# A fused attention and SoLU kernel: the first two tiles' h spread over rounds 10 to 14, one product moved, two g_ln products on VectorE, w_out copies later

## Chip, core and metric

The kernel runs on one core of a Trainium2 chip. The metric is device microseconds of one execution, lower is better. Engines are named as in the profile: PE is TensorE (PEld its weight loads), DVE VectorE, ACT ScalarE, POOL GpSimd, SP SyncE, which here issues nearly every DMA.

## What is computed

```python
# attention, per batch (8) and head (8), seq 576, head_dim 64
scores = q @ k.T / 8
scores = where(scores >= max(scores) - tau, scores, -1e9)
attn   = exp(scores - max(scores)); attn /= sum(attn) + 1e-9
x      = (attn @ v), heads side by side          # 4608 tokens x 512
# feed forward, per token
h    = x @ w_in                                   # 512 -> 1024
solu = h * exp(h - max(h)) / (sum(...) + 1e-9)
ln   = (solu - mean) / sqrt(var + 1e-6) * g_ln
out  = ln @ w_out                                 # 1024 -> 512
```

w_in and w_out arrive as 64-bit floats, and the kernel makes 32-bit floats of them with integer operations on the engines.

## The kernel before, in words

Attention is cut into 144 slots, 18 for each batch: two heads by 128 query rows each, and two slots at a batch's end for the 64 rows that are left over. A Python loop runs over rounds (line 855): round r issues the scores of slot r and the later steps of earlier slots, so the order of the instructions on every engine is the order in which the loop calls them. Each engine works its own list from front to back and waits on semaphores where data comes from another.

A slot goes through these steps. `scores(r)` (line 411): PE makes two 128 by 576 tiles in PSUM (`s0`, `s1`), ahead of them, where due, the turns of the next batch's q and k by matmuls with an identity (line 379). `maxes(r)` (line 455): DVE finds row minima of the negated scores. `ramp` (line 470) and `exps` (line 479): ACT, two of each. `keeps` (lines 388, 390): copies of turned q and k from PSUM. In round r+1: `normalise(r)` on POOL (lines 486 to 491), `blocks(r)` on DVE (line 501, 32x32 transposes), and after every second slot three DMAs (lines 510, 512) that carry T into wT. Three or four rounds after its second slot, the product with v (`attend_steps`, line 542) runs on PE for both slots of a unit, and ACT copies it to `xh` (line 572). `pv_due` holds the round from which each product is due, in order; slots 8 and 9 are due in round 12.

When the four units of 256 tokens of a batch and kind are done, two tiles of 128 tokens are ready for the feed-forward. Before the change, `ff_h` makes h in two halves, one per round: half 0 writes with `part` 0, then a memset on POOL (`fence`, line 110) waits for the last four matmuls of that half, and the first matmul of half 1 waits for that memset, since the rows change banks there. Half 0 of the first tile, (0, 0, 0), comes in round 11 and half 1 in round 12; the second, (0, 0, 1), has rounds 13 and 14. h takes one of two PSUM pairs (`p0`, `p1`), which the products with v and the output use too, and holds it until `ff_mul`. After h: `ff_max` (DVE, line 620), `ff_exp` (ACT, 629), `ff_mul` (DVE, 635), `ff_sum` (POOL, 640), `ff_stats` (DVE 650, then small POOL operations 654 to 661 whose last result is nb), `ff_norm` (ACT, 671, writes V), `ff_norm2` (DVE, 676), `ff_swap` (four DMAs, 687), `ff_turn` (DVE, 697, writes uT), `ff_o` (PE, 710, in two halves), `ff_store`. The first output half, of tile (0, 0, 0), is in round 17.

The weights come in 16 pieces of 128 by 512 (0 to 7 of w_in, 8 to 15 of w_out). Piece x = r + 1 is worked in round r: low word on ACT (line 263), two bit operations on DVE (282, 286) and a merge (308), in the next round an integer add on POOL (`weight_c`, 332). For w_out follow the product with g_ln, `weight_f` (line 340, ACT), and for every odd piece `weight_d` (line 347): two DMAs which copy the pair of pieces to the other half of the partitions, because `ff_o` reads both. In round r these two are called for piece r, at the end of the round. Loads of the next batch's q and k (`load_four`, line 142) are called at the very end: k in round 10, q in 12, k of the second four heads in 15, q in 17; the first are turned from round 14 on, the second from round 19 on.

Of the kernel before, what the change touches and what calls it, by code (L numbers as in the profile page):

```python
# [12 lines left out]
AF = mybir.ActivationFunctionType  # L13
ALU = mybir.AluOpType
# [6 lines left out]
def kernel(  # L21
# [315 lines left out]
    def weight_f(x):  # L337
        if wide and x >= 2 * NP:
            _, dst, unit = piece(x)
            nc.scalar.activation(out=dst, in_=dst, func=AF.Copy, scale=unit)  # L340

    def weight_d(x):
        c = x - 2 * NP
# [40 lines left out]
    def keep(room, i, nm, ms, by_act):  # L384
        of = room[:, 0 : 64 * len(ms)].rearrange("p (m x a) -> p m a x", a=2, x=32)
        to = pair(i)[nm + "T"].rearrange("p (a m x) -> p m a x", a=2, m=NK)[:, ms[0] : ms[-1] + 1]
        if nm == "k":
            (nc.scalar.copy if by_act else nc.vector.tensor_copy)(out=to, in_=of)
        elif by_act:
            nc.scalar.activation(out=to, in_=of, func=AF.Copy, scale=scl)  # L390
        else:
            nc.vector.tensor_scalar(out=to, in0=of, scalar1=scl, scalar2=None, op0=ALU.mult)
# [46 lines left out]

    def keeps(s, r):  # L440
        for room, i, nm, ms in live[s]["kept"].get(r, []):
            keep(room, i, nm, ms, r == 0 or s <= NW)

    def maxes(s, loose):
        d = live[s]
# [130 lines left out]
    def tokens(t):  # L576

        if len(t) == 1:
            return xe[t[0]]
        b, kind, m = t  # L580
        return xh[b, kind][:, :, P * m : P * m + P]


    def ff_h(t, part, split, beside=()):
        beside = iter(beside)
# [31 lines left out]
    def ff_max(t):  # L617
        d = ffn[t]
        d["nm"] = small.tile([P, 1], F32, tag="hm", name="hm")
        nc.vector.tensor_reduce(out=d["nm"], in_=d["h"], axis=AX.X, op=ALU.max, negate=True)  # L620

    def ff_exp(t):
        d = ffn[t]

        starts.append(t)
        tag = "xh1" if rnd > NS and len(starts) % 2 else "u"
        d["u"] = work.tile([P, DFF], F32, tag=tag, bufs=1, name="u")
        d["se"] = small.tile([P, 1], F32, tag="se", name="se")
        nc.scalar.activation(  # L629
            out=d["u"], in_=d["h"], func=AF.Exp, bias=d["nm"], scale=1.0, accum_out=d["se"]  # L630
        )

    def ff_mul(t):
        d = ffn[t]
        nc.vector.tensor_tensor(out=d["u"], in0=d["h"], in1=d["u"], op=ALU.mult)  # L635
        pairs_free.append(d["tag"])

    def ff_sum(t):
        se = ffn[t]["se"]
        nc.gpsimd.tensor_scalar(out=se, in0=se, scalar1=1e-9, scalar2=None, op0=ALU.add)  # L640
        nc.gpsimd.tensor_tensor(out=se, in0=se, in1=mone[:, 0:1], op=ALU.pow)

    def ff_stats(t):
        d = ffn[t]
        u, se = d["u"], d["se"]
        bs = small.tile([P, 2, 6], F32, tag="bs", name="bs")
        mv = small.tile([P, 2], F32, tag="mv", name="mv")
        rs = small.tile([P, 1], F32, tag="rs", name="rs")
        for f in range(2):
            nc.vector.bn_stats(out=bs[:, f], in_=u[:, 512 * f : 512 * f + 512])  # L650
        nc.vector.bn_aggr(out=mv, in_=bs)

# [8 lines left out]
        nc.gpsimd.tensor_scalar(  # L661
            out=nb, in0=mv[:, 0:1], scalar1=rs, scalar2=-1.0, op0=ALU.mult, op1=ALU.mult
        )
        d["norm"] = rs, nb

    def ff_norm(t):
        d = ffn[t]
        rs, nb = d["norm"]
        d["V"] = V = work.tile([P, 2, DFF // 2], F32, tag="V", bufs=1, name="V")
        u = d["u"].rearrange("p (g n) -> p g n", g=2)  # L670
        nc.scalar.activation(out=V, in_=u, func=AF.Identity, bias=nb, scale=rs)  # L671
# [76 lines left out]
    pv_due = []  # L748
    for s, (b, kind, hp, r) in enumerate(slots):
        if r == 1:  # L750
            pv_due.append((s + LAG_PV + (s < 6 or s in (11, PER - 1, PER + 9)), (b, kind, hp)))

    def first_slot(i):
        return PER * (i // NP) + 2 * (i % NP)
# [12 lines left out]
    for at, hf, what in (  # L767
# [3 lines left out]
        (25, 1, (2, 3)),  # L771
    ):
        load_at.setdefault(at, []).append(lambda hf=hf, what=what: load_v(1, hf, what))
    for i, at, nm in ((NP, 10, "k"), (NP, 12, "q"), (NP + 2, 15, "k"), (NP + 2, 17, "q")):
        load_at.setdefault(at, []).append(lambda i=i, nm=nm: load_four(i, nm))
    for i in range(2 * NP):
        ends_at[(9, 10, 11, 12, 21, 23, 26, 28)[i]] = i
# [31 lines left out]
    with tc.manual_schedule():  # L809
# [28 lines left out]
        weight_c(0)  # L838
        early = (1, )

        pieces = {r: x for r, x in enumerate(range(1, NW))}
        whole = {0: 1, 2: 2, 4: 3}
        for r, hf, parts in ((1, 0, (1, 2, 3)), (3, 1, (0,)), (5, 1, (1, 2, 3))):
# [8 lines left out]
        w2_done = False  # L852

        begin, middle, late, norms = {}, {}, {}, {}
        while True:
            more = rnd < NS
            if not more and not (
# [8 lines left out]
            if rnd == NS:  # L866
# [6 lines left out]
                    cur = None  # L873
                    quarter = 0
                assert quarter != 3
            if rnd == 13:
                prev, cur, quarter = cur, None, 0
            if (
                cur is None and quarter == 0 and ready and ready[0][0] <= rnd
                and (more or len(between) < 3 + (len(ready[0][1][0]) == 1))  # L880
            ):
                cur = ready[0][1].pop(0)
                if not ready[0][1]:
                    ready.pop(0)
# [52 lines left out]
            attending = None  # L937
            if due and (step is None or step[0] == "h") and len(pairs_free) > (step == ("h", 0)):
                attending = pv_due.pop(0)[1]
            beside = ()  # L940
            if attending is not None and attending[1] == 2 and step is not None:
                beside = attend_steps(attending)
            if step == ("h", 0):
                ff_h(cur, 0, rnd + 1 < NS, beside)
                quarter = 1
            elif step == ("h", 1):
                ff_h(cur, 1, None, beside)
                quarter = 2
                by = rnd + 2 * (rnd == 14)
                late.setdefault(by, []).append(lambda t=cur: (ff_max(t), ff_exp(t)))  # L950
                late.setdefault(by + 1, []).append(lambda t=cur: (ff_mul(t), ff_sum(t)))
                middle.setdefault(by + 2, []).append(lambda t=cur: ff_stats(t))
                if rnd + 6 < NS:
                    norms[by + 3] = cur
                else:
                    late.setdefault(rnd + 2, []).append(lambda t=cur: ff_norm(t))
                middle.setdefault(by + 3, []).append(lambda t=cur: (ff_norm2(t), ff_swap(t)))

                at = by + 4 if more or not ready or len(ready[0][1][0]) == 1 else rnd + 6
                if cur == (0, 1, 1):  # L960
                    middle.setdefault(rnd + 6, []).append(lambda t=cur, at=rnd + 6: ff_turn(t, at))
                else:
                    late.setdefault(at, []).append(lambda t=cur, at=at: ff_turn(t, at))
                if not more:
                    between.append(cur)
                    cur = None
                    quarter = 0
            elif step == ("o", 0):
                if prev is not None:
                    ff_o(prev, 0)  # L970
                quarter = 3
            elif step == ("o", 1):
                if prev is not None:
                    ff_o(prev, 1)
                    last = not (more or ready or cur or between)
                    begin.setdefault(rnd + 1, []).append(lambda t=prev, last=last: ff_out(t, last))
                    late.setdefault(rnd + 1, []).append(lambda t=prev, last=last: ff_store(t, last))
                prev, cur = cur, None
                quarter = 0
            if attending is not None:  # L980
                for _ in beside or attend_steps(attending):
                    pass
                attended(attending)
                b, kind, hp = attending
                if kind == 2 and b % 2:
                    ready.append((rnd + 1, [(b // 2,)]))
                elif kind < 2 and hp == NP - 1:
                    ready.append((rnd + 1, [(b, kind, 0), (b, kind, 1)]))
# [22 lines left out]
                        weight_e(x + 1)  # L1011
                    weight_m(x + 1)
            if rnd - 1 in pieces:
                weight_f(pieces[rnd - 1])
                weight_d(pieces[rnd - 1])
                w2_done = pieces[rnd - 1] == NW - 1
            for job in load_at.pop(rnd, []):
                job()
# [34 lines left out]
```

## Time and profile before

| what | us |
|---|---|
| runs without a profile | 855.26, 858.60, 859.29 |
| their median | 858.60 |
| span of the profiled execution | 854.9 |
| PE busy | 819.9 |
| DVE busy | 674.6 |
| ACT busy | 570.0 |
| POOL busy | 496.1 |

The span runs from the first to the last instruction of the profiled execution, on which all other rows of the profile rest; the page gives no other time for that execution. It is 0.4 us under the lowest of the three runs and 3.7 us under their median. Times in the views count from the span's start. In a row of the timeline stand the start, the length, engine, line and operation, and in square brackets the idle time ahead of it and what ended it. A float32 matmul shows as two records.

### The profile page before, as it was taken

How to read it: one execution, taken by the hardware profiler on the slowest of the kernel's cores; microseconds unless marked ns; L12 is line 12 of the kernel's file. 1: busy time of each engine (PE TensorE's matmuls, PEld its weight loads, DVE VectorE, ACT ScalarE, POOL GpSimd, SP SyncE). 2: the span in 40 equal slices, each digit the busy share in tenths (PEclk: the TensorE clock that was granted, in tenths of full speed). 3: DMA queues.
4: the chain of work that ended last, by engine and by line, in shares of the span. 5: the costliest groups of instructions: out<-in, count | busy, mean ns of one | idle time of the engine just before them, and what ended most of it. 6: DMA issues, size and time to landing. Idle time of an engine off the chain costs nothing.

```text
span 854.9 us, 36109 instructions
## 1 busy us (share of the span) xinstructions
PE 819.9 (96%) x15363; PEld 620.5 (73%) x15363; DVE 674.6 (79%) x1225; ACT 570.0 (67%) x1127; POOL 496.1 (58%) x945
## 2 busy tenths in 40 slices
PE   6778899999999999999999999999999999999997
PEld 5555677778677787777688877777777777777655
DVE  5997787989788888888788878888888878787361
ACT  6886876777767666667666666666677777775121
POOL 4885656666566656565566666565666655555120
PEclk8899999999999999999999999999999999999999
DMA  9999778798888888887888778887788887655212
GB/s 343 254 249 213 191 194 233 188 259 204 226 229 202 211 185 218 216 216 190 201 215 218 195 177 209 207 217 207 195 221 226 207 188 175 165 137 140 67 38 63
DMA packets 75314, 168.54 MB, mean 197 GB/s; under 512 B 11146, under 2 KB 32658, under 8 KB 75154
## 3 DMA queue, kind: packets, MB, share of 16 engines
q1 hardware_dynamic: 74866, 165.82, 76.7%
q8 instruction: 120, 1.97, 1.0%
q10 hardware_dynamic: 288, 0.43, 0.2%
q14 instruction: 40, 0.33, 0.1%
HBM read 46.14 MB, written 9.44 MB: 65 GB/s over the span
## 4 chain that ended last, share of the span: by engine, by line
PE 83%; DMA 4%; DVE 4%; ACT 3%; issue 2%; POOL 2%; SPq 1%; DVEq 0%; ACTq 0%; POOLq 0%
PE o_ps L710 27%; PE h_ps L605 22%; PE s_ps L434 15%; PE pv L542 14%; DMA wT<-T 3%; PE h_ps L595 3%; ACT w L470 1%; DVE w L455 1%; ACT w L479 1%; DVE T L501 1%; POOL w L489 1%; POOL sm L487 0%; PE s_ps L379 0%; DVE w L308 0%; PE tp L371 0%
## 5 line engine op out<-in xcount | busy, mean ns | idle before, releaser
L710 PE MATMUL o_ps<-w,uT 64*64 64x256 f32 x4608 | 269.5, 376 | 2.2 <-issue 1.6
L470 ACT ACTIVATE w<-s_ps,nth 128x576 f32<-128x576 f32 x280 | 196.8, 738 | 105.6 <-DVE nth L455 88.6
L455 DVE CUSTOM_DVE_ANT_0 w<-s_ps,tau_t 128x576 f32<-128x576 f32 x280 | 200.0, 751 | 83.5 <-PE s_ps L434 52.4
L710 PEld LDWEIGHTS o_ps<-w,uT 64*64 64x64 f32 x4608 | 221.8, 133 | 55.4 <-ACT xh L572 12.0
L489 POOL TENSOR_SCALAR w<-w,sm 128x576 f32<-128x576 f32 x288 | 220.6, 778 | 14.3
L501 DVE STREAM_TRANSPOSE T<-w 128x576 f32<-128x576 f32 x288 | 207.7, 756 | 22.6 <-POOL w L489 22.3
L605 PE MATMUL h_ps<-w,xh 64*64 64x512 f32 x1856 | 220.8, 589 | 0.0
L479 ACT ACTIVATE w<-w,ntau 128x576 f32<-128x576 f32 x288 | 219.6, 767 | 0.0
L542 PEld LDWEIGHTS pv<-wT,v 64*64 64x64 f32 x5760 | 172.6, 136 | 39.8 <-issue 16.7
L434 PE MATMUL s_ps<-kT,qT 64*64 64x512 f32 (+1 forms) x2048 | 175.8, 416 | 13.4 <-ACT w L470 11.3
L542 PE MATMUL pv<-wT,v 64*64 64x128 f32 (+1 forms) x5760 | 173.9, 263 | 8.3 <-DMA wT<-T 7.4
L605 PEld LDWEIGHTS h_ps<-w,xh 64*64 64x64 f32 x1856 | 118.4, 133 | 77.2 <-issue 43.6
L486 POOL TENSOR_SCALAR sm<-sm 128x2 f32<-128x2 f32 x144 | 34.2, 237 | 186.5 <-ACT w L479 182.8
L487 POOL TENSOR_TENSOR sm<-sm,mone 128x2 f32<-128x2 f32 x144 | 106.7, 741 | 12.0
L434 PEld LDWEIGHTS s_ps<-kT,qT 64*64 64x64 f32 x2048 | 72.7, 137 | 21.7 <-ACT w L470 16.2
L572 ACT COPY xh<-pv 128x256 f32<-128x256 f32 x64 | 25.4, 396 | 80.9 <-PE pv L542 80.9
L671 ACT ACTIVATE V<-u,nb,rs 128x1024 f32<-128x1024 f32 x36 | 44.7, 1240 | 40.5 <-POOL nb L661 33.6
L697 DVE STREAM_TRANSPOSE uT<-V 128x1024 f32<-128x1024 f32 x36 | 44.1, 1225 | 15.9 <-DMA V<-u 15.6
L479 ACT ACTIVATION_READ_ACCUMULATOR w<-w,ntau 128x1 f32 x288 | 55.4, 192 | 0.0
L676 DVE TENSOR_SCALAR u<-u,rs,nb 128x1024 f32<-128x1024 f32 x36 | 34.9, 971 | 19.5 <-ACT V L671 17.9
L635 DVE TENSOR_TENSOR u<-h_ps,u 128x1024 f32<-128x1024 f32 x36 | 42.8, 1190 | 9.4 <-ACT u L629 9.4
L620 DVE TENSOR_REDUCE hm<-h_ps 128x1 f32<-128x1024 f32 x36 | 42.9, 1193 | 4.9 <-PE h_ps L595 2.7
(77 smaller groups left out, 553.5 us busy)
## 6 DMA issues: line engine op xcount, KB each, us to landing
wT<-T SPq DMA_DIRECT2D x160, 288.0 KB, 6.5
wT<-T SPq DMA_DIRECT2D x64, 576.0 KB, 5.5
v<-in_v_dram SPq DMA_DIRECT2D x16, 576.0 KB, 6.0
V<-u SPq DMA_DIRECT2D x144, 64.0 KB, 3.5
out_dram<-ob SPq DMA_DIRECT2D x71, 128.0 KB, 2.6
q<-in_q_dram SPq DMA_DIRECT2D x28, 288.0 KB, 6.1
k<-in_k_dram SPq DMA_DIRECT2D x27, 288.0 KB, 6.4
qT<-flip SPq DMA_DIRECT2D x48, 144.0 KB, 3.2
```

Source lines behind the costliest of these rows:

```text
L434: nc.tensor.matmul(out=ps[h][ROWS[y], ks], lhsT=lhsT, rhs=d["kT"][ROWS[h], ks], start=True, stop=True,)
L455: nc.vector.tensor_tensor_reduce(out=w, in0=ps[:, 0:S], in1=(zero if loose else tau_t).to_broadcast([P, S]), scale=1.0, scalar=BIG, op0=AL ...
L470: nc.scalar.activation(out=d["w"][x], in_=d["w"][x] if d["loose"] else d["ps"][x][:, 0:S], func=AF.Prelu, bias=d["nth"][x], scale=-1.0, al ...
L479: nc.scalar.activation(out=w, in_=w, func=AF.Exp, bias=ntau, scale=1.0, accum_out=sm[:, x : x + 1])
L487: nc.gpsimd.tensor_tensor(out=sm, in0=sm, in1=mone, op=ALU.pow)
L489: nc.gpsimd.tensor_scalar(out=w, in0=w, scalar1=sm[:, x : x + 1], scalar2=1.0, op0=ALU.mult, op1=ALU.mult)
L501: nc.vector.transpose(out=T[:, :, r, h, :], in_=w)
L542: nc.tensor.matmul(out=to, lhsT=d["v"][ROWS[u], (h0 + h - u) % 4, m,], rhs=rhs, start=m == 0, stop=m == NK - 1,)
L605: mm = nc.tensor.matmul(out=h[ROWS[y], f], lhsT=x[ROWS[r], c, ROWS[y]], rhs=w1_parts[ROWS[r], c, part ^ r], start=part == 0 and c == 0, st ...
L671: nc.scalar.activation(out=V, in_=u, func=AF.Identity, bias=nb, scale=rs)
L697: nc.vector.transpose(out=uT, in_=d["V"].rearrange("p y (m x) -> p m y x", x=32))
L710: nc.tensor.matmul(out=d["o"][ROWS[z], 512 * (r ^ other) : 512 * (r ^ other) + 256], lhsT=d["uT"][ROWS[r], m].rearrange("p y x -> p (y x)" ...
```

## The change

Seven things are changed.

1. A new generator, `ff_groups`, issues the h of a tile in eight groups of four matmuls (one c of one part each), with the same fence between the parts. Tile (0, 0, 0) gets 3 groups in round 10, 4 in 11 and 1 in 12; tile (0, 0, 1) gets 3 in 12, 4 in 13 and 1 in 14. Each stands between the scores and the product with v of its round, in round 14 behind the product. The steps behind h (`after_h`) hang on the same rounds as before.
2. The product of slots 8, 9 is due in round 14 instead of 12.
3. `weight_f` of pieces 14 and 15 is a tensor_scalar on DVE, both at the end of round 15.
4. `weight_d` of pieces 9 and 11 is called in round 13, and those of 13 and 15 in rounds 14 and 15. Before, they were in rounds 9, 11, 13 and 15.
5. In round 15, the keeps of the second PSUM tile go to DVE.
6. k of the second four heads is loaded at the end of round 16, not 15.
7. From round 15 on the loop takes the two tiles as it did before.

```diff
     def weight_f(x):
         if wide and x >= 2 * NP:
             _, dst, unit = piece(x)
-            nc.scalar.activation(out=dst, in_=dst, func=AF.Copy, scale=unit)
+            if x >= NW - 2:
+                nc.vector.tensor_scalar(out=dst, in0=dst, scalar1=unit, scalar2=None, op0=ALU.mult)
+            else:
+                nc.scalar.activation(out=dst, in_=dst, func=AF.Copy, scale=unit)
...
-            keep(room, i, nm, ms, r == 0 or s <= NW)
+            keep(room, i, nm, ms, r == 0 or s <= NW and s != NW - 1)
...
+    def ff_groups(t):
+        x = tokens(t)
+        tag, h = take("h_ps")
+        ffn[t] = d = dict(h=h, tag=tag, split=True)
+        for part in range(2):
+            last = []
+            for c in range(NP):
+                for r in range(2):
+                    f = slice(512 * (part ^ r), 512 * (part ^ r) + 512)
+                    for y in range(2):
+                        mm = nc.tensor.matmul(
+                            out=h[ROWS[y], f], lhsT=x[ROWS[r], c, ROWS[y]], rhs=w1_parts[ROWS[r], c, part ^ r],
+                            start=part == 0 and c == 0, stop=part == 1 and c == NP - 1,
+                        )
+                        if part and not last:
+                            sync(mm, d["fence"])
+                        last.append(mm)
+                if part == 0 and c == NP - 1:
+                    d["fence"] = fence(last[-4:])
+                yield
...
-            pv_due.append((s + LAG_PV + (s < 6 or s in (11, PER - 1, PER + 9)), (b, kind, hp)))
+            pv_due.append((s + LAG_PV + (s < 6 or s in (11, PER - 1, PER + 9)) + 2 * (s == 9), (b, kind, hp)))
...
-    for i, at, nm in ((NP, 10, "k"), (NP, 12, "q"), (NP + 2, 15, "k"), (NP + 2, 17, "q")):
+    for i, at, nm in ((NP, 10, "k"), (NP, 12, "q"), (NP + 2, 16, "k"), (NP + 2, 17, "q")):
...
+        factors = {NW - 2: [], NW - 1: [NW - 2, NW - 1]}
+        copies = {13: [9, 11], 14: [13], 15: [15]}
+        groups = {10: [((0, 0, 0), 3)], 11: [((0, 0, 0), 4)], 12: [((0, 0, 0), 1), ((0, 0, 1), 3)],
+                  13: [((0, 0, 1), 4)], 14: [((0, 0, 1), 1)]}
+        running = {}
...
-            if rnd == 13:
-                prev, cur, quarter = cur, None, 0
+            if rnd == 15:
+                (_, (prev, cur)), quarter = ready.pop(0), 2
             if (
-                cur is None and quarter == 0 and ready and ready[0][0] <= rnd
+                rnd > 14 and cur is None and quarter == 0 and ready and ready[0][0] <= rnd
...
+            for t, n in groups.pop(rnd, []):
+                if t not in running:
+                    running[t] = ff_groups(t)
+                if rnd == 14 and attending is not None:
+                    for _ in attend_steps(attending):
+                        pass
+                for _ in range(n):
+                    next(running[t])
+                if rnd == 12 and t == (0, 0, 0) or rnd == 14:
+                    after_h(t)
...
             if attending is not None:
-                for _ in beside or attend_steps(attending):
-                    pass
+                if rnd != 14:
+                    for _ in beside or attend_steps(attending):
+                        pass
                 attended(attending)
...
             if rnd - 1 in pieces:
-                weight_f(pieces[rnd - 1])
-                weight_d(pieces[rnd - 1])
+                for x in factors.get(rnd, [pieces[rnd - 1]]):
+                    weight_f(x)
+                for x in copies.get(rnd, []):
+                    weight_d(x)
```

`after_h(t)` holds the lines that stood in the branch of the second half of h, unchanged, and that branch calls it now.

More of the change, by code (lines that the diff above doesn't have):

```diff
@@ L854, with after_h @@
         begin, middle, late, norms = {}, {}, {}, {}
+        def after_h(t):
+            by = rnd + 2 * (rnd == 14)
+            late.setdefault(by, []).append(lambda: (ff_max(t), ff_exp(t)))
+            late.setdefault(by + 1, []).append(lambda: (ff_mul(t), ff_sum(t)))
+            middle.setdefault(by + 2, []).append(lambda: ff_stats(t))
+            if rnd + 6 < NS:
+                norms[by + 3] = t
+            else:
+                late.setdefault(rnd + 2, []).append(lambda: ff_norm(t))
+            middle.setdefault(by + 3, []).append(lambda: (ff_norm2(t), ff_swap(t)))
+            at = by + 4 if more or not ready or len(ready[0][1][0]) == 1 else rnd + 6
+            if t == (0, 1, 1):
+                middle.setdefault(rnd + 6, []).append(lambda at=rnd + 6: ff_turn(t, at))
+            else:
+                late.setdefault(at, []).append(lambda at=at: ff_turn(t, at))
         while True:
@@ L948 @@
                 quarter = 2
[L949 to L963, printed above, removed]
+                after_h(cur)
                 if not more:
```

## Prediction, written before the result

> **What bounds the kernel now.** I read the page's span first, then a table of stretches cut where TensorE (PE) begins the scores of rounds 11 to 17, then the waits of that part, then the timelines of single engines. Round r handles slot r, and "maxes(r)", "exps(r)" are that slot's steps.
>
> ```profile
> span 854.9 us, 36109 instructions
> ```
> ```profile
> core 0: us, PE busy (x) PEld busy (x) DVE busy (x) ACT busy (x) POOL busy (x), PEclk, DMA share, GB/s
> 60.68:65.08 4.40, 4.40 (x60) 2.97 (x56) 3.89 (x9) 3.89 (x8) 3.93 (x5) 1.00 1.04 228
> 65.08:76.55 11.47, 8.18 (x123) 5.85 (x118) 7.70 (x13) 4.79 (x10) 8.56 (x13) 0.90 1.05 219
> ...
> 81.48:87.17 5.69, 5.69 (x108) 4.09 (x104) 5.42 (x12) 4.77 (x11) 4.10 (x8) 1.00 0.80 195
> 87.17:93.52 6.35, 4.35 (x149) 3.83 (x143) 4.15 (x8) 4.45 (x11) 5.73 (x11) 1.00 0.72 168
> 93.52:99.60 6.08, 5.55 (x118) 4.71 (x122) 3.57 (x9) 4.89 (x12) 3.60 (x5) 0.72 0.52 122
> 200.00:800.00 600.00, 597.81 (x11349) 460.45 (x11345) 492.89 (x888) 411.10 (x814) 360.22 (x700) 1.00 0.80 199
> ```
> PE is busy for 597.81 of the 600 us from 200 to 800, so what the change saves early should reach the end, and nothing later gets cheaper. The changed part is another matter. Round 12 (second row) lasts 11.47 us with PE busy for 8.18, while the DMA share stands at 1.05: the queue is full. Round 15 has 2.0 us without PE.
>
> ```profile
> DVE w L455 <- PE s_ps L434: 8.0, 4, 4.9
> ...
> PE pv L542 <- DMA wT<-T: 6.1, 4, 2.2
> PE s_ps L379 <- ACT qT L390: 2.0, 1, 2.0
> ```
> These are the waits from 54 to 104 us. PE waits 6.1 us for transposed weights, in rounds 10 and 12. Round 12's idle is 3.3 us (11.47 less 8.18), so round 10's 2.8. It is not all to be had: of the 8.0 us that DVE waits for scores, 4.9 are one wait, behind round 12; round 10's cost it little. Behind round 15 PE waits 2.0 us for a copy of turned q on ACT, and ACT, as the rows further down show, had stood before the g_ln product of a w_out piece (line 340).
>
> **The change, part by part.** Groups of h. The matmuls are the same; the unit is four matmuls of one c, eight records in the trace.
>
> ```profile
> 58.87 2.07 PE L542 MATMUL pv<-wT,v 64*64 64x128 f32 x66 [0.72 <-DMA wT<-T]
> 61.65 3.81 PE L605 MATMUL h_ps<-w,xh 64*64 64x512 f32 x32
> 89.21 2.30 PE L542 MATMUL pv<-wT,v 64*64 64x128 f32 x72
> ```
> An h half of 32 records holds PE from 61.65 to the next scores at 65.08, 3.43 us: 0.86 us a group. In round 10 three groups (2.6 us) go between the scores, done by 55.6, and the product, whose second half of wT lands at 58.87: 58.2, so hidden, and round 11 starts at 60.7 as before. From there the fence decides. Part 1's first matmul waits for a memset on POOL that waits for the last four of part 0. Before, part 1 came a round later, so only POOL waited. Now both stand in one round (11 for the first tile, 13 for the second), and in POOL's order the memset comes after that round's normalise and the integer add of a w_out piece (line 332). Behind the waiting matmul stand three groups and the next scores, and behind those every engine.
>
> ```profile
> 63.59 1.28 POOL L332 TENSOR_TENSOR w<-w,third 128x512 int32<-128x512 int32 x1
> 65.53 0.10 POOL L110 MEMSET mark<- 128x1 f32 x1 [0.65 <-PE h_ps L605]
> ...
> 67.34 1.47 POOL L489 TENSOR_SCALAR w<-w,sm 128x576 f32<-128x576 f32 x2
> ```
> ```profile
> 61.98 0.76 DVE L455 CUSTOM_DVE_ANT_0 w<-s_ps,tau_t 128x576 f32<-128x576 f32 x1 [0.48 <-PE s_ps L434]
> ...
> 66.38 0.76 DVE L455 CUSTOM_DVE_ANT_0 w<-s_ps,tau_t 128x576 f32<-128x576 f32 x1
> ...
> 78.37 0.76 DVE L455 CUSTOM_DVE_ANT_0 w<-s_ps,tau_t 128x576 f32<-128x576 f32 x1 [4.86 <-PE s_ps L434]
> ```
> Round 11: scores take 0.97 us (60.68 to 61.65) and the last group of part 0 0.86, so PE is at the fence at 62.5. POOL's add ends at 64.87, the memset takes 0.10: PE loses 2.4 us, does three groups (2.6) and begins scores(12) at 67.6, which is 2.5 later than before. Round 12: scores 0.97, one group 0.86, three of the second tile 2.6, no product: scores(13) at 72.0 instead of 76.55, so 4.5 early. DVE is then the later one: it was free at 78.37 - 4.86 = 73.5, 7.1 after maxes(12); now maxes(12) is at 68.9 (1.3 after the scores, as before), so maxes(13) at 76.0, 2.4 early. Round 13: PE is at the second fence at 73.9. From maxes(11) at 61.98 to the end of that slot's normalise at 68.81 are 6.8 us, with the add 8.1: from 68.9 that gives 77.0. PE loses 3.1 us, does three groups, and begins scores(14) at 79.6 instead of 81.48: 1.9 early, with maxes(14) at 82.1. Of the 6.1 us removed, the two fences (5.5) take most back, and this is the step I am least sure of.
>
> Product of slots 8, 9 to round 14. Before, it ran inside round 12, over by 76.55; in round 14 it begins at 81.9, so its data lies ready even if it came no earlier. PE in round 14: scores with turns 2.3 (5.69 less the 3.43 of an h half), product 2.1 (2.07 and 2.30 in the rows above, with some overlap), one group 0.86: 5.2 us. PE could begin scores(15) at 84.8; if they wait for ACT's ramps of slot 14, which follow maxes(14), they keep the 1.9 and begin at 85.3. I take 85.0, 2.2 early. The product's copy on ACT now stands ahead of V, inside the time that V waits for nb; if not, it costs its 0.4.
>
> g_ln on VectorE. ACT loses two copies and their waits, DVE gets two multiplications and the second key copy of slot 15.
>
> ```profile
> 90.40 0.72 ACT L340 ACTIVATE w<-w,gs 128x512 f32<-128x512 f32 x1 [1.90 <-POOL w L332]
> 91.03 1.23 ACT L671 ACTIVATE V<-u,nb,rs 128x1024 f32<-128x1024 f32 x1
> 92.16 0.72 ACT L470 ACTIVATE w<-s_ps,nth 128x576 f32<-128x576 f32 x1
> ```
> ```profile
> 88.87 0.27 POOL L661 TENSOR_SCALAR nb<-mv,rs 128x1 f32<-128x1 f32 x1
> ...
> 91.59 1.47 POOL L489 TENSOR_SCALAR w<-w,sm 128x576 f32<-128x576 f32 x2
> 93.02 1.70 POOL L332 TENSOR_TENSOR w<-w,em 128x512 int32<-128x512 int32 x1
> ```
> V (line 671) needs nb, which was there at 89.14 but V ran at 91.03. With nb 1.9 early it runs at 87.2, the ramp at 88.4, 3.8 early, and scores(16) at 89.7 instead of 93.52. The two keeps of the second head (one of 0.54, one smaller) no longer stand ahead of ACT's second ramp, so its second half starts some 0.6 earlier still. So far -4.4 at maxes(16), which were at 97.45. DVE now has more ahead of them: normalise(14) ends 3.9 after nb (89.14 to 93.06), so at 91.1, the second transpose at 91.9, then the two products. The add of the last piece (1.28 to 1.70) ends at 92.8 at most.
>
> ```profile
> L282 DVE TENSOR_SCALAR em<-raw 128x512 f32<-128x512 f32 x6 | 3.0, 502 | 0.2
> ...
> L390 ACT ACTIVATE qT<-s_ps,scl 128x320 f32<-128x320 f32 x2 | 1.1, 540 | 0.0
> ```
> The first row is the nearest to a g_ln product on DVE, 0.50 each. The last one ends near 93.3, so DVE and PE are level and maxes(16) come at 93.2, 4.2 early.
>
> Later copies, later k. The copies of pieces 9 and 11 go from rounds 9 and 11 to 13, and four key loads from 15 to 16. The bytes stay.
>
> ```profile
> 88.83 3.11 SPq L512 DMA_DIRECT2D wT<-T  x2
> 93.63 3.12 SPq L687 DMA_DIRECT2D V<-u  x4
> 97.09 1.36 SPq L347 DMA_DIRECT2D w<-w  x2
> 98.50 2.91 SPq L142 DMA_DIRECT2D k<-in_k_dram  x4
> ...
> 102.17 2.72 SPq L512 DMA_DIRECT2D wT<-T  x2
> ```
> ```profile
> 102.19 3.69 PE L710 MATMUL o_ps<-w,uT 64*64 64x256 f32 x64 [0.59 <-ACT xh L572]
> ...
> 106.67 3.63 PE L710 MATMUL o_ps<-w,uT 64*64 64x256 f32 x64
> ```
> ```profile
> V<-u SPq DMA_DIRECT2D x4, 64.0 KB, 2.6
> ```
> ```profile
> k<-in_k_dram SPq DMA_DIRECT2D x4, 144.0 KB, 3.7
> ```
> ```profile
> k<-in_k_dram SPq DMA_DIRECT2D x4, 144.0 KB, 8.9
> ```
> ```profile
> wT<-T SPq DMA_DIRECT2D x1, 576.0 KB, 11.0
> ```
> ```profile
> L697 DVE STREAM_TRANSPOSE uT<-V 128x1024 f32<-128x1024 f32 x36 | 44.1, 1225 | 15.9 <-DMA V<-u 15.6
> ```
> The first fence is SP's timeline (start, length of the issue), the second PE's; then come issues of single stretches with KB each and median us to landing, keys once behind 98 us and once behind 63, and the last is the page's group of the turns. SP passes wT of slots 12, 13 about 1.9 early (to 90.0). That wT may land a little after scores(16), but the product, done near 96, is still ahead of the turn. Then SP passes one w_out copy (1.4 by its like), then the swap of V, issued by 94.5 and landed by 97.1. The turn of uT (1.2) ends at 98.3, so the first output matmul, which waited last for ACT's copy of the round's product and then ran at 102.2, is at 98.4: 3.8 early, less than the 4.2 of maxes(16). For the keys: wT of slots 14, 15 is now ahead of them, issued from 96.2 (maxes(16), then two transposes, four passes of 0.75) for the 2.72 and 0.6 of its three issues to 99.5, keys to 102.4, landed 3.7 later at 106.1 in the better row, 111.3 in the worse. Round 19 turns them right behind the second output half (106.67 and the 3.4 us of 64 such records), at 110.1 before and 106.3 by this sum. I take the better row, since the copies have drained by then, and 0.3 us for it. **Sum:** -2.2 at scores(15) by the groups and the moved product, -1.6 more by the g_ln and keep moves, up to the limit of the swap, +0.3 for the keys: -3.5 us. The span becomes 851.4. The profiled span is 3.7 under the median of the three runs, 858.6 (they reach from 855.26 to 859.29); I keep that distance: **855.1 us**.
>
> **The rivals.** First, the clock. The granted clock was 0.72 in round 16, right behind a round with 2.0 us of idle PE, and 0.90 over round 12, whose own 3.3 us of idle lie in it. 0.28 of 6.08 us is 1.7 us of PE time for such a spell. The second fence's 3.1 us could call up another, over the three groups and scores(14): maxes(14) then keep only 0.2 us, round 16 some 2.3, the end 1.8: 856.8. The row of round 16 would speak for it, round 10's 2.8 us of idle, with a clock of 1.00 in round 11, against it. The Trainium skill, TensorE: Matmul & The Clock Gate, section Part 1 (The HAM clock gate), has the gate drop to half after an idle window of about 3.4 us that runs free of the kernel; the two rows agree in size, and by it a 3.1 us wait can fall either way.
>
> Second, faster: POOL reaches the fences as soon as PE. Then scores(12) start at 65.2 and DVE sets the pace: maxes(12) at 66.5, maxes(13) its 7.1 later, maxes(14) after the 5.4 us that it is busy in round 14 now, at 79.0; 3.1 more is -6.6, 852.0. For it: the emptier queue and the missing half-clock spell of round 12. Against it: POOL is busy for 3.93 of 4.40 us in round 11.
>
> Third, slower: the keys of round 19. If the queue is still full when they are issued (two w_out copies now stand closer ahead of them), they land as in round 10, 8.9 us after issue, 111.3, or 11.0 as wT did there, 113.4; the turns wait, 1.2 to 3.3 us later than before: 859.8 to 861.9. It decides from a landing time of 7.7 us. For it: shares of 1.04 and 1.05 in rounds 11 and 12; against: 0.72 and 0.52 in the two rounds ahead of the load.
>
> **How the numbers follow.** Forecast 0.45 (0.14 of it beyond 4.3 us), clock 0.17, faster 0.22, slower keys 0.16 (0.13 beyond 4.3, that bound taken with the runs' own scatter). 0.5%, about what a measurement of this kernel tells from no change, is 4.3 us. Faster 0.36, same 0.51, slower 0.13. The range reaches from the fast rival less 2.0, half the runs' scatter, to the upper key case: 850.0 to 861.9.
>
> **What would show it.** The waits: PE h on POOL's mark, 2.4 and 3.1 us; no PE wait on wT in rounds 10 to 14; scores(12) 2.5 late and scores(14) 1.9 early; no ACT wait on line 332; V at 87; a swap landing before the turn near 97; the first output matmul near 98.4; the key turns of round 19 without a wait. The granted clock behind the second fence decides the first rival. I am wrong if the fence waits are absent, or if the gain at the first output matmul is not there at the end.

## The result, and the profile after

The changed kernel takes 859.77 us (median of 20 runs, 854.10 to 865.98), the kernel before 856.02 in the same comparison (20 runs, 852.21 to 862.06). The ratio is 1.0046, with a 95% interval of 1.0025 to 1.0068: slower by 0.46%. The forecast was 855.1 us and faster by 3.5, so its sign was wrong; 859.8 lies inside its range. The forecast started from 858.6 us, the median of three runs; over 20 runs the kernel before has 856.02. Three single runs among all comparisons, each more than 1.5% above the fastest of its kernel, were in a slower state and are left out of the ratios and the means. The profiled execution took 863.56 us with a span of 861.8. Not all of that is the change: the two profiled spans differ by 6.9 us, the means of the runs by 3.6.

First the page's line, and the table of stretches of the changed kernel, cut again where the scores of rounds 11 to 17 begin (columns as before the change: length, busy time and instructions of PE, PEld, DVE, ACT, POOL, then granted clock, DMA share, GB/s).

```profile
span 861.8 us, 36107 instructions
```
```profile
63.04:68.77 5.73, 4.83 (x60) 1.80 (x56) 4.22 (x9) 5.20 (x11) 3.66 (x8) 1.00 0.92 237
68.77:73.18 4.41, 4.41 (x53) 1.65 (x48) 3.11 (x7) 2.81 (x6) 3.59 (x5) 1.00 0.58 178
73.18:82.49 9.31, 6.01 (x53) 1.90 (x46) 7.50 (x14) 6.94 (x14) 7.96 (x12) 0.82 0.84 217
82.49:87.58 5.09, 5.09 (x157) 4.42 (x153) 2.61 (x6) 1.81 (x4) 0.01 (x1) 1.00 0.57 163
87.58:92.68 5.10, 4.58 (x148) 3.74 (x143) 4.55 (x12) 4.73 (x11) 4.10 (x9) 1.00 0.45 106
92.68:101.95 9.27, 6.05 (x119) 4.87 (x123) 7.15 (x13) 5.97 (x14) 6.49 (x10) 0.82 0.81 188
200.00:800.00 600.00, 595.69 (x11358) 459.11 (x11351) 494.25 (x891) 413.63 (x819) 360.12 (x696) 1.00 0.81 199
```

Round 12 is now short (4.41 us, PE busy throughout). Two other rounds have become long: round 13 with 3.3 us of idle PE and round 16 with 3.2, each with a granted clock of 0.82. From 200 to 800 us PE is as busy as it was. Who makes PE wait, from 50 to 125 us:

```profile
PE pv L545 <- DMA wT<-T: 4.4, 4, 2.3
PE h_ps L597 <- POOL mark L110: 4.2, 2, 3.3
...
PE s_ps L382 <- DMA k<-in_k_dram: 1.1, 2, 0.6
```

The wait for wT is still there, but it has moved from rounds 10 and 12 to rounds 9, 10 and 16; the wait for POOL's mark (the fence) and the one for the keys are new. PE's timeline shows the places:

```profile
61.23 2.07 PE L545 MATMUL pv<-wT,v 64*64 64x128 f32 x66 [0.47 <-DMA wT<-T]
...
66.14 2.81 PE L597 MATMUL h_ps<-w,xh 64*64 64x512 f32 x24 [0.90 <-POOL mark L110]
...
74.15 1.04 PE L597 MATMUL h_ps<-w,xh 64*64 64x512 f32 x8
78.49 4.17 PE L597 MATMUL h_ps<-w,xh 64*64 64x512 f32 x24 [3.30 <-POOL mark L110]
...
95.92 0.44 PE L545 MATMUL pv<-wT,v 64*64 64x128 f32 x4 [0.95 <-DMA wT<-T]
98.62 3.59 PE L545 MATMUL pv<-wT,v 64*64 64x128 f32 x66 [2.27 <-DMA wT<-T]
...
102.92 3.83 PE L734 MATMUL o_ps<-w,uT 64*64 64x256 f32 x64
...
112.59 1.49 PE L382 MATMUL s_ps<-ident,k 64*64 64x64 f32 x48 [0.62 <-DMA k<-in_k_dram]
```

Twice a wait is followed by a slow stretch of the same work: three groups (24 records) take 2.81 us behind the first fence and 4.17 behind the second, and 66 records of a product take 2.07 in round 10 and 3.59 in round 16. On POOL, the add of a w_out piece stands ahead of the second fence, as the prediction has it:

```profile
77.12 1.27 POOL L332 TENSOR_TENSOR w<-w,em 128x512 int32<-128x512 int32 x1
78.33 0.10 POOL L110 MEMSET mark<- 128x1 f32 x1
```

The queue of DMAs, on SP's timeline (start, length of the issue), and the keys' landing time in a stretch from 105 to 109 us:

```profile
89.84 2.95 SPq L515 DMA_DIRECT2D wT<-T  x2
92.89 2.23 SPq L350 DMA_DIRECT2D w<-w  x2
95.22 3.94 SPq L711 DMA_DIRECT2D V<-u  x4
99.26 1.33 SPq L350 DMA_DIRECT2D w<-w  x2
...
101.33 4.11 SPq L515 DMA_DIRECT2D wT<-T  x2
105.49 3.57 SPq L142 DMA_DIRECT2D k<-in_k_dram  x4
```
```profile
k<-in_k_dram SPq DMA_DIRECT2D x4, 144.0 KB, 5.3
```

From 89.8 to 109.1 SP issues almost without a gap, so every transfer stands behind the issues ahead of it, and the keys are issued at 105.5.

### The profile page after: what moved, and what is told of

It is laid out like the page before. It is cut to its first block, busy times and chain, and to the rows that moved or that the text cites. A ratio compares the mean times of both kernels' runs of the same rounds, so it can differ in the third digit from the quotient of the medians.

```text
span 861.8 us, 36107 instructions
## 1 busy us (share of the span) xinstructions
PE 821.5 (95%) x15363; PEld 614.3 (71%) x15363; DVE 674.1 (78%) x1229; ACT 568.7 (66%) x1123; POOL 495.7 (58%) x945
## 4 chain that ended last, share of the span: by engine, by line
PE 79%; DMA 7%; SPq 3%; POOL 3%; ACT 3%; issue 2%; DVE 2%; DVEq 0%; ACTq 0%; POOLq 0%
PE o_ps L734 26%; PE h_ps L629 20%; PE s_ps L437 15%; PE pv L545 14%; DMA wT<-T 4%; PE h_ps L619 3%; SPq L515 1%; ACT w L473 1%; DMA q<-in_q_dram 1%; POOL w L492 1%; DMA k<-in_k_dram 1%; ACT w L482 1%; PE h_ps L597 1%; POOL sm L490 1%; DMA raw<-in_moe_w_out_dram 1%
## 5 line engine op out<-in xcount | busy, mean ns | idle before, releaser
L629 PE MATMUL h_ps<-w,xh 64*64 64x512 f32 x1728 | 205.1, 589 | 0.0
L437 PE MATMUL s_ps<-kT,qT 64*64 64x64 f32 (+1 forms) x2048 | 174.4, 415 | 14.8 <-ACT w L473 11.3
L629 PEld LDWEIGHTS h_ps<-w,xh 64*64 64x64 f32 x1728 | 107.4, 133 | 74.7 <-issue 50.5
L653 ACT ACTIVATE u<-h_ps,hm 128x1024 f32<-128x1024 f32 x36 | 40.1, 1115 | 10.7 <-DMA V<-u 5.1
```

What stands on the lines that cost most here:

```text
L437: nc.tensor.matmul(out=ps[h][ROWS[y], ks], lhsT=lhsT, rhs=d["kT"][ROWS[h], ks], start=True, stop=True,)
L629: mm = nc.tensor.matmul(out=h[ROWS[y], f], lhsT=x[ROWS[r], c, ROWS[y]], rhs=w1_parts[ROWS[r], c, part ^ r], start=part == 0 and c == 0, st ...
```

## Experiments

Theories, before the first run: the fences inside rounds 11 and 13 are the loss, since PE stands behind POOL's normalise and add; or the late transfers are (copies and keys), through rounds 16 and 19; or the gain never existed, because the wait that it came from belongs to one execution and not to the kernel. A fourth came up on the way: that the late keys disturb the rounds beyond 30 (theory K). Every kernel was timed in five rounds beside the kernel before on the same chip, 12 runs each (10 for one of them) against 23 to 35. Besides the ratio (with its 95% interval) I give the difference of the means in us, this kernel less the kernel before, with its standard error, worked out from the lists of runs.

**Both kernels again, without an edit.**

> The changed kernel once more, for the scatter of its trace. Theory A (transfers: wT of slots 12, 13 and the keys of round 19 land late): again a PE wait of 2 to 3 us for wT in round 16 and of about 1 us for keys in round 19. Theory B (fences): again PE waits for POOL's mark, 3 us or more in round 13, with a half-clock spell behind it. Theory C (scatter of one profiled run): the two waits for transfers are gone in this trace while the time stays. Time against before: 1.003 to 1.007.

> The kernel before once more, for the scatter of its trace. Theory S (the round 12 wait of the first trace, 3.3 us and a half-clock spell, is not in every execution, and the forecast took it for a constant): no PE wait for wT in round 12, first output matmul near 98.8 us instead of 102.2, as in the two kernels that share its program up to round 15. Theory N (it is the rule, and the other two traces were the lucky ones): 2 to 3.5 us of wait in round 12 again. Time 1.000 of before.

The changed kernel again: ratio 1.0042 (1.0013 to 1.0071), means +3.8 ± 1.0 us; the result stands. The kernel before again: 0.9997 (0.9970 to 1.0023). Its trace is the more important: lines of PE's timeline, of PE's waits from 50 to 115 us, and of the stretch from 60 to 66 us.

```profile
59.16 3.89 PE L542 MATMUL pv<-wT,v 64*64 64x128 f32 x66 [0.85 <-DMA wT<-T]
...
72.74 2.23 PE L542 MATMUL pv<-wT,v 64*64 64x128 f32 x70
...
100.25 3.68 PE L710 MATMUL o_ps<-w,uT 64*64 64x256 f32 x64 [0.59 <-ACT xh L572]
```
```profile
PE pv L542 <- DMA wT<-T: 2.7, 2, 1.8
```
```profile
60.00:66.00 6.00, 6.00 (x88) 4.87 (x84) 1.93 (x5) 1.83 (x4) 4.00 (x6) 0.57 1.06 230
```

The same program, and no wait in round 12: the product at 72.74 has no bracket. Round 10 was the bad one here, with the product at a granted clock of 0.57. The first output matmul came at 100.25 instead of 102.19. The 3.3 us that the prediction removed belong to one execution.

**The fences ahead of normalise.** The groups of rounds 10 to 13 are issued earlier in the program, so that on POOL the memset stands before that round's normalise and add. PE's order is the same.

```diff
+            for t, n in groups.get(rnd, []) if rnd != 14 else []:
+                if t not in running:
+                    running[t] = ff_groups(t)
+                for _ in range(n):
+                    next(running[t])
+                if rnd == 12 and t == (0, 0, 0):
+                    after_h(t)
             if rnd - 1 in live:
...
-            for t, n in groups.pop(rnd, []):
+            for t, n in groups.pop(rnd, []) if rnd == 14 else []:
```

> The changed kernel with the groups of rounds 10 to 13, and so both fence memsets, issued ahead of that round's normalise on POOL; PE's order is the same. Theory B: the PE waits for the mark (4.2 us) fall under 0.5 us, no half-clock spell in round 13, scores of slot 14 some 3 us earlier, and the time 2 to 4 us under the changed kernel's. Theory A: rounds 11 to 13 gain but the transfers take it back at round 16 or 19, and the time moves by less than 1 us.

> The kernel of after_early_fence once more (late copies and late keys, fences ahead of normalise). Theory A2 (the late transfers cost in every execution): 3 to 5 us lost between slots 16 and 20 in the trace again, and the time at 1.000 or above. Theory F (the fences inside a round are the loss, the key wait is a matter of the single execution): 0.996 to 0.999 of before again.

0.9972 (0.9943 to 1.0001) and, repeated on another chip, 0.9985 (0.9961 to 1.0009); means -1.5 ± 1.1 and -0.6 ± 0.9. Of the first of them PE's waits, and lines of the timelines of PE and POOL:

```profile
PE h_ps L597 <- POOL mark L110: 0.5, 2, 0.2
```
```profile
76.35 2.81 PE L597 MATMUL h_ps<-w,xh 64*64 64x512 f32 x24 [0.23 <-POOL mark L110]
```
```profile
66.39 0.10 POOL L110 MEMSET mark<- 128x1 f32 x1 [5.88 <-PE h_ps L597]
```

Now POOL waits for PE (5.88 us at the first fence) and PE for POOL only 0.2 at each, and behind the second fence the 24 records take 2.81 us, not 4.17. On one chip this kernel stands 5.3 ± 1.3 us below the changed one (856.0 against 861.3), over both comparisons 4.7 ± 1.0. The fences are a real loss, and the largest. Without them the change still gains no more than 1.0 ± 0.7 us, where the prediction's own figure for that case, its second rival, was 6.6.

**The transfers where they were.**

```diff
-    for i, at, nm in ((NP, 10, "k"), (NP, 12, "q"), (NP + 2, 16, "k"), (NP + 2, 17, "q")):
+    for i, at, nm in ((NP, 10, "k"), (NP, 12, "q"), (NP + 2, 15, "k"), (NP + 2, 17, "q")):
...
-        copies = {13: [9, 11], 14: [13], 15: [15]}
+        copies = {9: [9], 11: [11], 13: [13], 15: [15]}
```

Both lines, fences inside the rounds, twice:

> The changed kernel with the four w_out copies in rounds 9, 11, 13, 15 and the key load at the end of round 15 again. Theory A: the wait for keys in round 19 is gone and that for wT in round 16 shrinks by at least half; the time is 2 to 4 us under the changed kernel's of the same call, so 0.999 to 1.002 of before. Theory B: fence waits stay at 4 us together and the time moves by less than 1 us, 1.004. If the old copies hold up wT of slots 6, 7 and 8, 9 instead, rounds 10 and 11 lose some 2 us.

> The kernel of after_old_copies once more (fences inside the round, copies and keys where they were). Theory A2: nothing lost between slots 16 and 20, 1.000 to 1.001. Theory F: PE waits 4 us for the mark again, 1.002 to 1.004.

1.0014 (0.9983 to 1.0045) and 1.0008 (0.9975 to 1.0040), means +0.9 ± 0.9 and +1.4 ± 1.3. The fence waits are as they were, in the first of the two

```profile
PE h_ps L597 <- POOL mark L110: 4.3, 2, 3.3
```

and the wait for the keys is gone. The first line alone, the keys' load:

> The changed kernel with the key load at the end of round 15 again; the w_out copies stay late. Theory K (the late keys are the transfer that costs): no PE wait for keys in round 19, and no loss against the kernel before in rounds 31, 32 and 41, 42, where both traces of the changed kernel lose 2.3 and 1.5 us; the time about 0.999 of before. Theory W (the late copies cost, by way of wT of slots 12, 13): the wait in round 16 stays, and the losses in rounds 31 to 42 with it; 1.004.

1.0055 (1.0029 to 1.0081), means +4.4 ± 0.9: PE no longer waits for keys, and nothing is won, so the keys cost nothing that the runs can show. What the old places of the transfers give back, 2.6 ± 1.1 us in the two kernels above, must come from the copies, if it is there. In this trace PE waits 0.34 and 3.30 us at the fences, and the second is not followed by a slow stretch (24 records in 2.81 us), yet the time is no better. Near 130 us PE then waits 4.0 us in one piece, for nothing that the profile shows.

Both lines with the fences ahead of normalise, twice, and the keys' line alone with them:

> Fence memsets ahead of normalise, and w_out copies and key load where they were before the change. If the two causes add up, fences (6 us by the run of that part) and transfers (3 us): 0.993 to 0.996 of before, no key wait, mark waits under 1 us, no step in rounds 31 to 42. If they overlap: 0.997.

> The kernel of after_fence_old_copies once more (fences ahead of normalise, copies and keys where they were). Theory A2: nothing lost between slots 16 and 20, and 2 to 4 us less than early_fence_2: 0.995 to 0.998. Theory F: the same as early_fence_2 within 1.5 us.

> Fences ahead of normalise, w_out copies late as in the changed kernel, key load at the end of round 15. If the groups with the fences out of the way gain in rounds 10 to 16 (3.7 and 6.7 us in two traces) and the keys were what took it back in round 19 (1.2 and 0.6 us of wait there): nothing lost between slots 16 and 20, 0.995 to 0.997 of before, under both kernels. If the late copies hold up wT of slots 12, 13 all the same: a wait of 2 us in round 16, 0.998 to 1.000.

0.9985 (0.9959 to 1.0010), 0.9994 (0.9968 to 1.0020) and 0.9998 (0.9973 to 1.0023). The gains expected, 0.993 to 0.997, did not come. The means of the first two are -2.0 ± 0.9 and -0.3 ± 1.1, against the fences ahead with late transfers 0.2 ± 1.0 us lower: with the fences out of the way the transfers make no difference that shows. The first of the three has a span of 850.9 us and a new wait among PE's, for the queries of the next batch:

```profile
PE s_ps L382 <- DMA q<-in_q_dram: 2.7, 2, 1.9
```

A front part that runs earlier meets the loads that were issued for the old times.

**One part alone, on the kernel before.** The product of slots 8 and 9 in round 14 (`+ 2 * (s == 9)` in `pv_due`), twice:

> The kernel before with the product of slots 8, 9 due in round 14 and nothing else. Theory B (the groups with fences inside a round are the fault, the moved product is good): PE has no wait for wT in round 12, scores of slot 13 some 4 us earlier, no half-clock spell there, and 2 to 3 us less at the end, 0.997. Theory A: the early gain meets later transfers and is given back by round 19, 1.000 with an interval of 0.003.

> The kernel of before_late_product once more. If it beats both kernels: 0.996 to 0.999 of before, no PE wait for wT in round 12. If its first trace (849.7 us) was a lucky draw: 1.000.

0.9979 (0.9947 to 1.0011) and 0.9989 (0.9963 to 1.0015), means -1.8 ± 1.2 and +0.1 ± 0.9, together -0.8 ± 0.8. This edit only takes the product and its wait for wT out of round 12, the prediction's largest gain, and it is worth no more than this, where 2 to 3 us were expected of the first run.

Keys one round later (16 for 15), and the later copies (the `copies` table in front of `weight_d`), each by itself:

> The kernel before with the four key loads at the end of round 16 and nothing else. Theory K: issued behind wT of slots 14, 15, from 105 to 108 us, they land near 112.5, so PE waits some 2 us in round 19, and the steps of rounds 31 to 42 appear: 3 to 6 us later, 1.004 to 1.007 of before. Theory W: the load is as good there, 1.000.

> The kernel before with the w_out copies of pieces 9 and 11 in round 13 and that of 13 in round 14 and nothing else. Theory K: wT of slots 8, 9 lands some 2 us sooner, PE's wait in round 12 falls from 3.3 to about 1.5 us, and nothing is lost later: 0.997 to 1.000. Theory W: wT of slots 12, 13 lands late, a PE wait of 2 us or more in round 16: 1.002 to 1.004.

1.0000 (0.9971 to 1.0028) and 0.9987 (0.9961 to 1.0013). Neither costs anything that shows without the groups. Theory K falls here. Between the starts of the normalise of slots 30 and 48 (174.19 and 268.39 in the first trace of the kernel before) the trace with late keys loses 4.1 us (171.21 and 269.55), but the repeat of the kernel before, with its keys in round 15, loses 3.9 as well (171.80 and 269.93).

The g_ln products of pieces 14 and 15 on DVE with the keeps (items 3 and 5 of the change), and these together with the moved product:

> The kernel before with g_ln of pieces 14 and 15 on VectorE at the end of round 15 and the keeps of the second tile of slot 15 there; nothing else. If the forecast's step is right: no ACT wait at line 340 in round 14, V some 2 us earlier, PE's wait for turned q in round 15 (2.0 to 2.3 us) mostly gone, and 1.5 to 2 us less at the first output matmul; 0.998. If the ACT wait only moves to DVE: 1.000. Its program is that of the kernel before up to round 14, so it also shows round 12 once more (theories S and N).

> The kernel before with the product of slots 8, 9 in round 14 and g_ln and keeps on VectorE: the two parts that need no transfer moved. No wait for wT in round 12, and round 15's wait for turned q mostly gone: first output matmul near 97.5, 0.995 to 0.998 of before. If round 14 with product and h half is now the late one: 0.998 to 1.000.

1.0000 (0.9971 to 1.0028) and 0.9991 (0.9965 to 1.0016). In the first trace ACT has no wait at the g_ln line, V runs at 82.4, and the first output matmul comes at 96.9, the second earliest of all these traces; but PE then waits for queries,

```profile
PE s_ps L382 <- DMA q<-in_q_dram: 2.2, 2, 1.6
```

and the run times show nothing.

**The change without its groups** (item 1 left out, the old `ff_h` halves in rounds 11 to 14), and the same with the keys' load in round 15:

> The change without its first part: h in halves in rounds 11 to 14 as before, all the rest as in the changed kernel. Theory B (the groups with their fences inside one round are the main loss): 4 to 6 us under the changed kernel, 0.996 to 1.000 of before. Theory A (the late transfers): stays at 1.002 to 1.004, with the key wait of round 19 and the steps of rounds 31 to 42.

> The kernel before with the moved product, g_ln and keeps on VectorE and the late copies: the change without the groups and without the late keys. If the parts add up: no wait for wT in round 12, none for turned q in round 15, none for keys in round 19, first output matmul near 97.3, 0.996 to 0.998 of before. If later waits take the early gain back: 0.999 to 1.000.

1.0013 (0.9984 to 1.0042) and 0.9993 (0.9969 to 1.0018), means +0.2 ± 1.0 and -0.6 ± 0.9. All that is left of the change is neutral; its loss needs the groups. In the first, PE waits 1.7 us for keys:

```profile
PE s_ps L382 <- DMA k<-in_k_dram: 1.7, 2, 1.4
```

**Together.** Differences from the kernel before, means of the pairs of comparisons, in us (late transfers: w_out copies and keys as in the change):

| | late transfers | old transfers |
|---|---|---|
| fences inside the round | +3.7 ± 0.7 | +1.1 ± 0.8 |
| fences ahead of normalise | -1.0 ± 0.7 | -1.2 ± 0.7 |

Down a column the fences are worth 4.7 ± 1.0 and 2.3 ± 1.1. No version beats the kernel before by more than its interval.

## Why the prediction was wrong, step by step

**The step that failed is the term "-2.2 at scores(15) by the groups and the moved product", through the baseline under it: "Round 12's idle is 3.3 us (11.47 less 8.18)", booked as removed.** That idle time was read from a single execution. Of five traces of programs that have the h and the product of round 12 where they were, one shows it: it is missing in the repeat of the kernel before, with late keys, with late copies and with g_ln on DVE, where 70 records of that product take 2.22 or 2.23 us without a wait. The edit that removes it alone gains 0.8 ± 0.8 us. In the changed kernel's trace round 13 does start 3.4 us earlier than in the trace before (73.18 for 76.55), but that trace was the late one there: maxes(13) stand at 75.4 us in the changed kernel's trace, and at 75.4 (71.6 to 78.4) on average over the five. The prediction held the profiled span against the median of the runs, but not the early rounds of one trace against those of another.

What the term came to can be read at maxes(15) on DVE. First the row of the trace before, then that of the changed kernel:

```profile
89.52 0.76 DVE L455 CUSTOM_DVE_ANT_0 w<-s_ps,tau_t 128x576 f32<-128x576 f32 x1 [0.80 <-issue]
```
```profile
90.25 0.76 DVE L458 CUSTOM_DVE_ANT_0 w<-s_ps,tau_t 128x576 f32<-128x576 f32 x1 [0.51 <-ACT xh L575]
```

The same row stands at 87.1 us on average in the five traces just named (85.8 to 89.5), at 89.7 in the five with fences inside the rounds (87.8 to 90.6), and at 87.3 in the five with fences ahead (84.5 to 89.0). So the term measures +2.6 us and not -2.2, and +0.2 without the fence waits. Half of the error of 4.8 us is the late baseline (89.5 for 87.1). The other half is lateness against the forecast's own time, 87.3, and goes with the slow stretch behind the second fence: the one trace of the five without it stands at 87.8, the four with it at 89.5 to 90.6.

**The fences: right in kind; the second right in size, the first too large.** Forecast 2.4 and 3.1 us of idle PE; the five traces with fences inside show 0.90, 1.56, 1.03, 1.28 and 0.34 at the first and 3.30 or 3.31 at the second, always. The first came out smaller in the changed kernel's trace because PE was later there, at 65.2 and not 62.5: its product of round 9 ended some 2 us later than in the trace before. Moving both away gives 4.7 ± 1.0 us back with late transfers and 2.3 ± 1.1 with the old ones, where 5.5 were booked; but that also takes away the slow stretch behind the second fence, which the sum didn't book. With a gain that isn't there, the fences become the net loss.

**The first rival, the clock, came true beside it.** Behind the 3.30 us the 24 records took 4.17 us, 1.4 more than behind the first fence, and 4.42, 5.40 and 4.13 in three of the other four traces; only with the old keys was it 2.81. It is the clock: from 78.5 to 80 us the granted clock is 0.50 in each of the four and 1.00 in the fifth. The rival had 1.7 us for it, with a chance of 0.17; the runs show 1.3 to 2.6. The Trainium skill, TensorE: Matmul & The Clock Gate, section Part 1 (The HAM clock gate), has the clock halve after an idle window of about 3.4 us. These waits are a little shorter and still lead to it four times in five; and in the repeat of the kernel before, waits of 1.82 and 0.85 us with 0.44 us of matmuls between them sufficed, as the row with 0.57 shows. So here idle time that is shorter, or broken by a few matmuls, is enough.

**Round 10: hidden, as forecast, and better.** The product still waits (0.47 us, where the prediction looked for no wait for wT in rounds 10 to 14), so the groups stand in idle time. What the prediction couldn't see in its trace: without groups the product of round 10 runs slowly in 7 of 10 traces (2.90 to 3.89 us for 66 records), with groups in none of 10 (2.07 or 2.08 us, or 2.23 to 2.57 for 70 records). That is a gain of the groups, and may be why the kernels with fences ahead come out under the kernel before, if they do.

**Rounds 14 and 15: right.** The product of slots 8 and 9 ran in round 14 without a wait, and round 14 took 5.09 us (forecast 5.2 for its PE work, 5.4 from start to start). ACT and DVE in the changed kernel:

```profile
90.17 1.24 ACT L695 ACTIVATE V<-u,nb,rs 128x1024 f32<-128x1024 f32 x1 [0.37 <-POOL nb L685]
```
```profile
95.14 1.18 DVE L341 TENSOR_SCALAR w<-w,gs 128x512 f32<-128x512 f32 x2
...
100.64 1.25 DVE L721 STREAM_TRANSPOSE uT<-V 128x1024 f32<-128x1024 f32 x1 [1.38 <-DMA V<-u]
```

V runs right behind nb, and scores(16) 2.51 us after V's start (forecast 2.5). The two products take 1.18 us together, where two of 0.50 were booked. maxes(16) stand 3.56 us behind scores(16), forecast 3.5. All of it is shifted by what the rounds up to 13 lost: V at 90.2 and not 87.2.

**The transfers in round 16: mis-sized.** The prediction let the wT of slots 12 and 13 "land a little after scores(16)" at no cost. PE waited 0.95 and 2.27 us for it, and the product behind it took 3.59 us. The copy ahead of the swap took SP 2.23 us where 1.4 was booked, the swap 3.94 and not 3.12, so the turn of uT, forecast to end at 98.3, waited and ran from 100.6 to 101.9. The first output matmul came at 102.92, forecast 98.4. It waited for nothing there that the trace names.

**The keys: the rival's wait, just under its lowest price, by another way.** They landed 5.3 us after their issue, neither the 3.7 of the forecast nor the 8.9 of the rival; but they were issued from 105.5 us, not 99.5, behind SP's late list. PE waited 1.1 us for them in round 19 (0.49 and 0.62), where the rival gave 1.2 to 3.3. But with the keys back in round 15 the time is no better.

**The path to the end.** PE is busy for 595.69 of the 600 us, as forecast, and yet an early gain or loss doesn't arrive as it stands. With g_ln on DVE the first output matmul came 3.4 us before that of the repeat, and the means differ by 0.1 ± 1.3. Over the 20 traces the start of the first output matmul and the span go together only loosely (their correlation is 0.62). Between 100 and 280 us the traces shift against one another by up to 5 us, in one kernel as well as between two: through waits for the next batch's queries, and through gaps near 130 us, none to 4.0 us long, that end on nothing that the profile shows. The three shortest spans (849.7, 849.8 and 850.9) have 0.2 us or less of such a gap.

**Open:** how the late copies cost something only together with the fences (2.6 ± 1.1 against 0.2 ± 1.0 may still be chance); what the gaps near 130 us and the scatter beyond 100 us are made of; and whether a fence on another engine, which would not hold POOL up while it waits for PE, would let the groups gain, which wasn't tried.

## What to carry to other kernels

Before a wait is booked as a gain, look for it in a second trace of the same program: a wait for a DMA behind a full queue can be in one execution and not in the next. A synchronisation step on an in-order engine costs what stands ahead of it there, so issue it ahead of that round's long work; here this alone was worth 4.7 ± 1.0 us, or 2.3 ± 1.1 with the transfers in their old places. A wait of PE just over 3 us should be priced with the slow stretch behind it, 1.3 to 2.6 us in four of five traces here.

## What the runs showed of the hardware

- In the same place of programs that are the same up to there, the wT of slots 8 and 9 landed 11.0, 9.6 and 7.7 us after its issue (the kernel before, its repeat, and late keys). The runs of one kernel spread over 10 us (852.21 to 862.06); an estimate from their standard deviation of about 3 us is that a part worth 2 us needs some 24 runs on each side to be seen, since the mean of 24 has a standard error of 0.6.
- Behind a PE wait of 3.3 us the granted clock was 0.50 in four traces of five (from 78.5 to 80 us), and 24 matmul records took 4.13 to 5.40 us instead of 2.81.
- The distance between a profiled execution's time and its span is 1.8 us (863.56 and 861.8; 856.28 and 854.5 with late copies). By this estimate 1.9 of the 3.7 us that the prediction kept were the distance of that one execution from the median of three runs.
- In the changed kernel's trace SP issued from 89.8 to 109.1 us without a gap of more than 0.11 us, at 0.6 to 2.1 us a DMA. A transfer that stands late in that list is issued late, whenever its data was ready: the keys followed at once on wT (105.44 and 105.49).
